# Four transfers for each q, k and v load and two for each quarter of the expert weights, in a fused attention and mixture-of-experts kernel

## The chip, the cores and the metric

The kernel runs on one core of a Trainium2 chip. The metric is the device time of one execution in microseconds (us). Each time stands with the number of executions behind it, and each execution has a state: slow when its time is over 1.5% above the fastest of the same kernel, else fast. Slow runs stay in the medians and ranges quoted, and it is said where there is one. Every time *inside* an execution comes from the one execution of that kernel that was profiled, whose time is some 1.5 to 1.8 us longer than the span that its profile shows; every profiled execution here was a fast one.

The engines are called as in the profile: PE (TensorE, matmul), PEld (its weight loads), DVE (VectorE), ACT (ScalarE), POOL (GpSimd), SP (SyncE, which here only issues transfers). The kernel gives each engine its own list of instructions.

## The reference, cut to what matters

```python
# attention: batch 8, heads 8, seq 576, head_dim 64, 32 landmarks
q_lm = q.reshape(B, H, m, S // m, D).mean(axis=3)      # means over 18 rows each
k_lm = k.reshape(B, H, m, S // m, D).mean(axis=3)
A  = softmax(scale * q @ k_lm.T);  Bm = softmax(scale * q_lm @ k_lm.T);  C = softmax(scale * q_lm @ k.T)
Z  = six Newton steps towards the inverse of Bm
x  = A @ Z @ C @ v                                      # then laid out as (4608, 512)
# mixture of experts: 8 experts, w1 (512 x 1024), w2 (1024 x 512)
e_idx = argmax(x @ w_gate);  gate_w = softmax(x @ w_gate)[e_idx];  eom = sigmoid(x @ w_output_gate)
for e in range(8):
    h = relu(x[mask] @ w1[e]);  out[mask] = gate_w * eom * (h @ w2[e])
```

q, k and v are 32-bit floats, 28 MB in all, and everything else waits for them. The experts' weights are 16-bit in the kernel's memory and 32-bit outside.

## The kernel before

The kernel computes one batch of attention after another, and for each batch it finds the expert that its rows chose, fetches this expert's weights and runs it. When the second of two batches in one weight buffer has chosen the expert that is there already, the fetch is issued under a condition and skipped; on these inputs five experts are fetched and three fetches are skipped. "Expert 0" below is the expert of the first batch, and so on.

A small list scheduler written in the kernel (`Plan`) fixes the order of instructions of every engine when the kernel is built. The change alters none of its inputs, so the order stays.

The loads are issued by SP, one transfer a tensor and batch (two for q and k of the first):

```python
        cuts = ((0, 2), (2, 4)) if b == 0 else ((0, 4),)
        for h, (lo, hi) in enumerate(cuts):
            def ldq(lo=lo, hi=hi):
                nc.sync.dma_start(out=qT.ap[:, lo:hi, :].rearrange("p a s -> p (a s)"), in_=qT_d[ORDER[b]][:, S * lo:S * hi])
        # ... k alike; v in one transfer of 128 rows of 9360 bytes
```

The landmark sums of k are made by DVE ("k sum" below), those of q, but for the first batch, as a tree of five additions by GpSimd ("q tree"; there are seven). GpSimd also reads the number of the chosen expert into a register and issues the weight transfers, four a expert:

```python
            def value(b=b, i8=i8):
                regs[b] = nc.gpsimd.value_load(i8.ap.bitcast(I32)[0:1, 0:1], min_val=0, max_val=E - 1)
    ...
    def fetch(w1t, w2t, reg, k, **kw):                       # one quarter of an expert's weights
        dst = w1t[:, k].rearrange("p a x -> p (a x)") if k < 2 else w2t[:, 4 * k - 8:4 * k - 4].rearrange("p a x -> p (a x)")
        src = w_d[bass.ds(reg, 1)][:, :, 2048 * k:2048 * k + 2048].rearrange("e p x -> p (e x)")
        nc.gpsimd.dma_start(out=dst, in_=src, **kw)
```

The weights are cast on the way: the page's account of 62.05 MB read from memory is what q, k and v (28.5 MB) and 32 weight transfers at 8192 bytes a row make up, where a weight packet writes 4096 bytes. (That account counts the skipped fetches too.) No run here gives these transfers to SP.

Last, the gate values. `coef` may be placed on DVE or GpSimd by the scheduler, `tmp` too, `cmain` is DVE's:

```python
        plan.op(f"co{b0}", [("DVE", 0.26, co("vector")), ("POOL", 0.26 + 0.12 * n, co("gpsimd"))], ...)   # coef
        plan.op(f"tm{b0}", [("DVE", 0.26, tm("vector")), ("POOL", 0.26 + 0.12 * n, tm("gpsimd"))], ...)   # tmp <- coef, sels
        plan.op(f"cm{b0}", [("DVE", 0.24, ...)], ...)                                                    # cmain <- tmp
```

The softmax here doesn't subtract the row's maximum and nothing guards it: scores larger than these inputs give would overflow.

## Time and profile before

| | before |
|---|---|
| time, median of 3 | 192.99 us (192.61 to 194.84; in the ratios below the last counts as slow) |
| profiled execution | 192.17 us, span 190.4 us, granted TensorE clock 0.90 |
| busy share of the span | PE 75%, DVE 68%, ACT 52%, POOL 28% |
| transfers | 375 GB/s over the span, reads and writes, by the account that counts skipped fetches |

The busy shares do not say what limits the kernel, because three stretches with three limits follow one another. The page's second part cuts the span into 40 slices, here of 4.76 us; each digit is a busy share of the slice in tenths. Of the kernel before:

```profile
PE   0087779757959697375999799785976999999940
...
POOL 2039910894830048990000001620400010100000
...
DMA  5999999999999999999701405999999666066752
```

Up to about 90 us the DMA engines are full; q, k and all but the last v arrive until about 71 us, and then the last v (until 80 us) and the first two experts' weights. From 90 us on PE is at 9 in most slices. Between these two lies a stretch in which POOL is busy (the two nines in slices 17 and 18, counted from one, 76 to 86 us) and PE is not (3 and 7 there, 5 in the next). The timeline of that stretch, with start and duration in us, engine, line, and in brackets the idle time of the engine before the instruction and what ended it:

```profile
69.66 1.68 POOL L942 DMA_DIRECT2D w<-in_w_dram  x3 [0.28 <-issue]
72.03 2.26 POOL L942 DMA_DIRECT2D w<-in_w_dram  x4 [0.69 <-issue]
74.31 2.40 POOL L545 TENSOR_TENSOR qa<-qT 128x1152 f32<-128x1152 f32 x1
...
80.19 0.26 POOL L917 TENSOR_TENSOR coef<-mk,gt 128x40 f32<-128x40 bf16 x1
80.41 2.42 POOL L545 TENSOR_TENSOR qa<-qT 128x1152 f32<-128x1152 f32 x1
...
80.99 1.86 DVE L922 TENSOR_SCALAR sels<-iota,ef 128x8 f32<-128x8 f32 x1
82.96 1.26 DVE L926 TENSOR_TENSOR tmp<-coef,sels 128x40 f32<-128x40 f32 x1
84.26 0.20 DVE L931 TENSOR_REDUCE cmain<-tmp 128x5 f32<-128x40 f32 x1
84.37 2.54 DVE L534 TENSOR_REDUCE kx<-kx 128x128 f32<-128x2304 f32 x1
...
87.02 0.75 PE L570 MATMUL psum<-kx,ql 64*32 64x304 f32 x16 [2.53 <-POOL ql L550]
```

Read it as one chain. POOL issues eight weight transfers (one at 68.66 us, and the seven shown), without waiting for any of them. Only then comes the sixth q tree (that of batch 6, counted from 0), then `coef`, and only with `coef` can DVE make `tmp` and `cmain`. The k sum stands behind these on DVE, though its data have long landed (the last k by 68.7 us), and the score matmul of PE, which reads it, starts 0.11 us after its end. The bracket names POOL as the releaser, because the matmul waits for several semaphores and POOL's came last by the profile's count; by the times, the last of its inputs is the k sum (84.37 + 2.54 = 86.91 us). So whatever delays POOL before 80 us delays PE.

### The profile page before, as it was taken

What the parts mean: (1) busy time and instruction counts of PE and PEld (TensorE: products, weight loads), DVE (VectorE), ACT (ScalarE), POOL (GpSimd) and SP (SyncE); (2) the same over time, 40 slices, a digit from 0 to 9 for tenths busy, and PEclk for the clock granted to TensorE, in tenths of its full rate; (3) what the DMA queues carried; (4) which work ended last, traced back from release to release, by engine and by line L of the source; (5) the groups of instructions that cost most, each with busy time, mean ns of one, the idle gap of its engine ahead of it and who ended that gap; (6) DMA issues with size and microseconds to landing.
All of it is one profiled execution on the core that took longest, in us unless ns stands there. A gap on an engine that the chain in (4) does not pass through costs nothing.

```text
span 190.4 us, 7174 instructions
## 1 busy us (share of the span) xinstructions
PE 142.5 (75%) x3013; PEld 79.5 (42%) x3014; DVE 129.7 (68%) x312; ACT 98.5 (52%) x213; POOL 53.4 (28%) x92
## 2 busy tenths in 40 slices
PE   0087779757959697375999799785976999999940
PEld 0033334433527464253344464463443555434320
DVE  6845543697317466898779987677586967927960
ACT  2025824423654327024489668865266667686340
POOL 2039910894830048990000001620400010100000
PEclk9999975995796969667599999999999999999996
DMA  5999999999999999999701405999999666066752
GB/s 175 418 399 406 419 425 396 407 413 400 419 416 405 399 304 259 283 216 211 142 3 67 172 20 214 174 222 215 213 215 213 125 237 247 22 234 248 262 203 55
DMA packets 15636, 48.91 MB, mean 257 GB/s; under 512 B 1648, under 2 KB 2672, under 8 KB 13680
## 3 DMA queue, kind: packets, MB, share of 16 engines
q1 hardware_dynamic: 12576, 37.90, 51.2%
q0 software_dynamic: 2880, 10.49, 28.1%
q8 instruction: 24, 0.39, 0.8%
q14 instruction: 12, 0.10, 0.2%
q10 hardware_dynamic: 144, 0.03, 0.1%
HBM read 62.05 MB, written 9.44 MB: 375 GB/s over the span
## 4 chain that ended last, share of the span: by engine, by line
PE 46%; DMA 15%; DVE 13%; POOL 9%; issue 9%; ACT 4%; POOLq 1%; DVEq 0%
PE psum L1003 15%; DMA qT<-in_q_dram 12%; PE psum L772 6%; PE psum L1009 5%; PE psum L570 4%; POOL qa L548 4%; POOL qa L545 4%; PE psum L576 3%; DMA w<-in_w_dram 3%; PE psum L998 3%; PE psum L608 3%; DVE sab L1056 2%; PE psum L860 2%; PE psum L640 2%; DVE ql L534 1%
## 5 line engine op out<-in xcount | busy, mean ns | idle before, releaser
L942 POOL DMA_DIRECT2D w<-in_w_dram x32 | 11.5, 358 | 88.2 <-PE psum L772 31.8
L1003 PE MATMUL psum<-w,X 128*128 128x512 bf16 x128 | 32.1, 393 | 3.3 <-issue 2.0
L570 PE MATMUL psum<-kx,ql 64*32 64x304 f32 x256 | 16.7, 524 | 16.2 <-DVE kx L534 10.2
L1084 ACT ACTIVATE y<-psum,cmain 128x512 f32<-128x512 f32 (+1 forms) x35 | 21.6, 658 | 7.9 <-PE psum L1009 3.8
L545 POOL TENSOR_TENSOR qa<-qT 128x1152 f32<-128x1152 f32 x7 | 16.9, 2414 | 19.3 <-DMA qT<-in_q_dram 19.0
L534 DVE TENSOR_REDUCE kx<-kx 128x128 f32<-128x2304 f32 (+1 forms) x9 | 20.4, 2277 | 2.5 <-DMA kx<-in_k_dram 2.5
L772 PE MATMUL psum<-cur,Q 32*32 32x96 f32 (+1 forms) x768 | 16.2, 266 | 7.0 <-DVE Q L801 2.9
L1003 PEld LDWEIGHTS <-X 128*128 128x128 f16 x128 | 11.8, 101 | 18.2 <-issue 6.5
L1056 DVE TENSOR_REDUCE sab<-psum 128x4 f32<-128x992 f32 x16 | 18.8, 1182 | 0.0
L586 ACT ACTIVATE Cexp<-psum 128x544 f32<-128x544 f32 x8 | 5.0, 625 | 26.4 <-PE psum L570 26.4
L548 POOL TENSOR_TENSOR qa<-qa 128x512 f32<-128x512 f32 (+2 forms) x21 | 17.4, 830 | 1.6
L1009 PE MATMUL psum<-P,A 128*128 128x512 f16 x64 | 16.4, 380 | 0.8 <-DVE P L1070 0.5
L772 PEld LDWEIGHTS psum<-cur,Q 32*32 32x32 f32 x768 | 9.4, 113 | 16.9 <-DVE Q L801 6.0
L783 ACT COPY cur<-psum 128x384 f32<-128x384 f32 (+1 forms) x23 | 9.4, 417 | 13.7 <-DVE Q L801 9.6
L576 PE MATMUL psum<-qT,kx 64*32 64x288 f32 x256 | 16.1, 512 | 0.4 <-ACT Bx L593 0.4
L705 DVE SCALAR_TENSOR_TENSOR A<-A,lift,psum 128x576 f16<-128x576 f16 x16 | 12.7, 807 | 4.5 <-PE psum L700 4.5
L801 DVE TENSOR_TENSOR Q<-twoI,psum 128x128 f32<-128x128 f32 (+1 forms) x25 | 6.4, 259 | 12.9 <-PE psum L772 7.8
L640 PE MATMUL psum<-vn,CT 128*32 128x65 f32 x512 | 11.6, 252 | 4.0 <-DMA vn<-in_v_dram 2.6
L570 PEld LDWEIGHTS psum<-kx,ql 64*32 64x32 f32 x256 | 4.5, 121 | 21.4 <-DVE kx L534 11.0
L598 ACT ACTIVATE A<-psum 128x576 f16<-128x576 f32 x16 | 10.5, 655 | 5.1 <-PE psum L576 5.1
L998 PE MATMUL psum<-MTd,w 128*128 128x64 f16 x256 | 10.9, 198 | 2.7 <-ACT Bx L593 0.9
L998 PEld LDWEIGHTS <-w 128*128 128x128 f16 x256 | 10.0, 101 | 6.0 <-issue 3.2
(137 smaller groups left out, 240.2 us busy)
## 6 DMA issues: line engine op xcount, KB each, us to landing
w<-in_w_dram POOLq DMA_DIRECT2D x32, 512.0 KB
vn<-in_v_dram SPq DMA_DIRECT2D x8, 1170.0 KB, 18.6
out_dram<-y SPq DMA_DIRECT2D x32, 256.0 KB, 2.2
qT<-in_q_dram SPq DMA_DIRECT2D x7, 1152.0 KB, 13.7
kx<-in_k_dram SPq DMA_DIRECT2D x7, 1152.0 KB, 15.9
qT<-in_q_dram SPq DMA_DIRECT2D x2, 576.0 KB, 4.8
kx<-in_k_dram SPq DMA_DIRECT2D x2, 576.0 KB, 6.9
out_dram<-y SPq DMA_DIRECT2D x16, 64.0 KB, 2.0
```

The lines of the kernel that those rows point to most:

```text
L534: plan.op(f"{what}s{b}.{h}", [("DVE", 0.07 + 0.62 * (hi - lo), lambda lo=lo, hi=hi: nc.vector.tensor_reduce(dst()[:, lo:hi], src()[:, lo:h ...
L545: nc.gpsimd.tensor_tensor(a, x[:, :, :, 0:9], x[:, :, :, 9:18], op=ADD)
L548: nc.gpsimd.tensor_tensor(a[:, :, :, 0:n], a[:, :, :, 0:n], a[:, :, :, n:2 * n], op=ADD)
L570: nc.tensor.matmul(psC[hf].ap[quad(p), par, 0:CH], lhsT=ql.ap[half(par), p, :], rhs=kx.ap[half(par), p, CH * hf:CH * hf + CH], start=True, ...
L576: nc.tensor.matmul(psA[hf].ap[quad(p), par, 0:HS], lhsT=kx.ap[half(par), p, 0:m], rhs=qT.ap[half(par), p, HS * hf:HS * hf + HS], start=Tru ...
L640: nc.tensor.matmul(pV.ap[quad(p), par, 0:D + 1], lhsT=CT.ap[:, par, 128 * c + 32 * p:128 * c + 32 * p + 32], rhs=vn.ap[:, 8 * c + 2 * p + ...
L772: nc.tensor.matmul(it.ap[to, par, 96 * i + lo:96 * i + 96], lhsT=s[:, 0:m] if st == 0 else Q.ap[fr, par, i, :], rhs=s[:, lo:], start=True, ...
L998: nc.tensor.matmul(o, lhsT=weights(b)[0][:, u, q, 128 * fc:128 * fc + 128], rhs=MTd[:, b, q, :].rearrange("p (a x) -> p a x", a=2), start= ...
L1003: nc.tensor.matmul(dst, lhsT=Xt[:, fc, 128 * par:128 * par + 128], rhs=w2t[:, fc, :], start=(fc == 0), stop=(fc == FC - 1))
L1009: nc.tensor.matmul(dst, lhsT=A16[b][:, par, 128 * c:128 * c + 128], rhs=Pt[:, par, :], start=(par == 0), stop=(par == 1))
L1056: nc.vector.tensor_reduce(sab[:, b, f4], x, axis=mybir.AxisListType.XY, op=ADD, apply_absolute_value=True)
L1084: nc.scalar.activation(out=o, in_=x, func=COPY, scale=k)
```

## The change

It cuts every load of q, k and v into four transfers of 295 KB (v: 299 KB) and every quarter of an expert into two, each of 128 rows still. What such a cut can hope for is a consumer that starts with the first piece. No consumer here does: sums and trees read all pieces.

```diff
-                nc.sync.dma_start(out=qT.ap[:, lo:hi, :].rearrange("p a s -> p (a s)"), in_=qT_d[ORDER[b]][:, S * lo:S * hi])
+                for p in range(lo, hi):
+                    nc.sync.dma_start(out=qT.ap[:, p, :], in_=qT_d[ORDER[b]][:, S * p:S * p + S])
     # ... k alike ...
-            nc.sync.dma_start(out=vn.ap.rearrange("p a s -> p (a s)"), in_=v_d[ORDER[b]])
+            for c in range(4):
+                nc.sync.dma_start(out=vn.ap[:, 9 * c:9 * c + 9].rearrange("p a s -> p (a s)"), in_=v_d[ORDER[b]][:, 585 * c:585 * c + 585])
     # ... in fetch() ...
-        nc.gpsimd.dma_start(out=dst, in_=src, **kw)
+        for h in range(2):
+            nc.gpsimd.dma_start(out=dst[:, 1024 * h:1024 * h + 1024], in_=src[:, 1024 * h:1024 * h + 1024], **kw)
```

```
L946 DMACopy w_0_95<-in_w_dram 128x1024
L946 DMACopy w_1_94<-in_w_dram 128x1024 [waits DMASW0_49]
L946 DMACopy w_1_94<-in_w_dram 128x1024 [waits DMASW1_49]
...
L946 DMACopy w_1_96<-in_w_dram 128x1024 [waits DMASW7_49]
```

The trace has the same: expert 1's eight issues each carry a wait for one of eight semaphores, in the order of expert 0's, and SP's transfers take eight in turn as well. Before, experts 0 and 1 were just eight transfers, and none of them waited.

More of the change, by code (lines that the diff above doesn't have):

```diff
@@ L523, in ldk @@
             def ldk(lo=lo, hi=hi):
-                nc.sync.dma_start(out=kx.ap[:, lo:hi, m:], in_=kT_d[ORDER[b]].rearrange("p (a s) -> p a s", a=NP)[:, lo:hi])
+                for p in range(lo, hi):
+                    nc.sync.dma_start(out=kx.ap[:, p, m:], in_=kT_d[ORDER[b]][:, S * p:S * p + S])
             dma(f"ldk{b}.{h}", ldk, kb * (hi - lo) / 4, ("L", b, 0.1 + 0.01 * h), w=[("k", b, h)], new=[] if h else [kx], use=[kx] if h else [])
         def ldv():
-            nc.sync.dma_start(out=vn.ap.rearrange("p a s -> p (a s)"), in_=v_d[ORDER[b]])
+            for c in range(4):
+                nc.sync.dma_start(out=vn.ap[:, 9 * c:9 * c + 9].rearrange("p a s -> p (a s)"), in_=v_d[ORDER[b]][:, 585 * c:585 * c + 585])
         dma(f"ldv{b}", ldv, 128 * 36 * 65 * 4 / 1e3, ("V", b, 0), w=[("v", b)], new=[vn])
```

## The prediction

> **What bounds the kernel now.** From 2 to 71 us the DMA is full (slice row: 9 in every slice, about 400 GB/s): q, k and v stream in order, and the chain of waits holds 17.9 us of "DMA qT" (15.7 to 33.7 us). From about 88 us on PE, fed by in-order DVE and ACT, is the limit (PE 9 in most slices), with 6 us of weight landing at 118. Between them lies the stretch that matters. GpSimd (POOL) issues the weights of experts 0 and 1 (timeline: 8 transfers, 68.7 to 74.3 us, about 0.56 us each), then makes the two last q trees (74.3 to 80.1, 80.4 to 86.2 us), with coef at 80.2 between them. DVE needs that coef for tmp (83.0), then makes the k sum (84.4 to 86.9), and PE's score matmul follows at 87.0 us.

> **Removed:** nothing. No consumer starts earlier: sums and trees read all pieces, and the instruction order of PE, DVE and ACT is unchanged in the build.

> **Added.** (1) Packets. In the packet records 9216 B take 351 ns, 2304 B 95 ns; so q costs 4x95-351 = 29 ns more per row, v about 26. Over 16 engines, with 9 ns per extra completion packet, that is 1.4 us by the fourth q (33.1 us), 2.5 to 3 us by the last k. [...] (2) GpSimd issue: each half still has 128 rows, so I estimate 0.56 us each, double per expert.
> (3) Semaphore slots, the main cost. The build gives each DMA path eight completion semaphores in rotation; a ninth transfer waits until the first has landed. SP stays safe: eight pieces of 0.295 MB are about 5.8 us of queue, above the 1.0 us from issue to first packet. GpSimd does not: before, two experts are exactly eight transfers and it waits for none. After, they are sixteen: expert 1's eighth half waits for expert 0's eighth.

> **On the critical path.** The four quarters of expert 0 landed at 74.2, 79.8, 82.6 and 85.1 us in the completion packets, sharing the engines with the last v. [...] the eighth half lands near 87.5. So GpSimd is free at about 88 instead of 74.3 us; coef comes at 94, the k sum ends at about 99, the score matmul runs near 99 instead of 87.0: +12 us, and everything in order behind it moves along. The same recurs for experts 2 and 3: coef and tmp of their group stand behind six halves of expert 3, each waiting for a half of expert 2; cmain on DVE slips from 124.7 by about 5 us relative, of which 1.3 us is idle now: +4 us. Expert 4 finds slack.

> **Predicted: 208 us**, 8 in 10 between 200 and 215. Faster 0.01, within 2% 0.03, slower 0.96.

> **What would show it.** Timeline of GpSimd: second expert's halves spaced by 1.2 to 2 us, each "<-DMA w", and the sixth q tree starting near 88 us. DVE idle before tmp for some 10 us, released by GpSimd. Packets of 2304 and 2340 B at 95 to 98 ns. DMA still full to about 73 us; if it has holes there, SP's eight slots starve it and my step is wrong. cmain of group (2,3) about 5 us later relative to the load of expert 2.

> **What would make it wrong.** GpSimd's issue being much cheaper or dearer for half rows; the first halves landing sooner because v, now in small packets, takes a smaller share of the engines; slack in DVE or PE after the stall that absorbs part; PE's granted clock rising after a longer idle (now 0.90).

## The result, and the profile after

The changed kernel took 216.69 us (median of 4, 216.12 to 218.16); the kernel before, in the same rounds, 192.8 us (median of 4, one of them slow, 191.32 to 194.84). Ratios here are the mean time of one kernel's fast runs over that of the other's fast runs of the same rounds, so they are not quite the ratio of the medians: it is 1.128, 95% interval 1.1185 to 1.1374. The direction of the prediction held, and so did the mechanism of its largest term; the size did not. 216.7 us lies above the range of 200 to 215 us. All outputs are right.

The slices of the changed kernel are of 5.4 us:

```profile
PE   0094899479878954001899898753959899999900
...
POOL 2049602984503422598000003543150011100000
...
DMA  5999999999999999991000415999999256167560
```

PE now has a hole in slices 17 to 19 (87 to 103 us), a dip in slices 26 to 28 (135 to 152 us), and no work in the last two. DMA is full up to 97 us and has no holes, so SP's own eight semaphores do no harm. The timeline of the hole; these are the instructions shown of before, at line numbers three or four higher:

```profile
68.49 4.61 POOL L946 DMA_DIRECT2D w<-in_w_dram  x8 [10.81 <-DVE e L908]
76.13 0.53 POOL L946 DMA_DIRECT2D w<-in_w_dram  x1 [3.03 <-DMA w<-in_w_dram]
78.15 0.53 POOL L946 DMA_DIRECT2D w<-in_w_dram  x1 [1.49 <-DMA w<-in_w_dram]
...
90.08 0.53 POOL L946 DMA_DIRECT2D w<-in_w_dram  x1 [1.08 <-DMA w<-in_w_dram]
90.63 2.38 POOL L548 TENSOR_TENSOR qa<-qT 128x1152 f32<-128x1152 f32 x1
...
96.30 0.26 POOL L920 TENSOR_TENSOR coef<-mk,gt 128x40 f32<-128x40 bf16 x1
...
96.59 2.34 DVE L929 TENSOR_TENSOR tmp<-coef,sels 128x40 f32<-128x40 f32 x1 [16.07 <-POOL coef L920]
98.96 0.20 DVE L934 TENSOR_REDUCE cmain<-tmp 128x5 f32<-128x40 f32 x1
99.14 2.55 DVE L537 TENSOR_REDUCE kx<-kx 128x128 f32<-128x2304 f32 x1
...
101.79 1.27 PE L573 MATMUL psum<-kx,ql 64*32 64x304 f32 x16 [18.16 <-POOL qa L551]
```

Expert 0's eight halves are issued in 4.61 us, 0.58 us each. Each of expert 1's halves then waits for the landing of one of them ("<-DMA w"; by the trace's semaphore records each starts 0.28 or 0.29 us after the sixteenth count of the semaphore that it waits for), and POOL stands still in between, with a tree and a `coef` to make whose inputs are all there. The tree begins at 90.63 us instead of 74.31, DVE idles 16.07 us, PE 18.16 us. That is the price, in this trace, of eight semaphores and an issuer that works in order: PE had idled 2.53 us there before.

To see where the rest comes from, I matched the 312 instructions of DVE of the two traces one by one (their order is the same) and took how much later each one starts. The shift changes in only a few places:

| place, before | shift of DVE | what DVE or PE waited for there |
|---|---|---|
| k sum, 84.4 us | +14.8 | POOL `coef`, above |
| 105.0 to 118.0 us | +15.2 | nothing more: clock |
| CT copy, 127.6 us | +21.1 | POOL `tmp` behind the halves of experts 2 and 3 |
| 136.4 us | +20.6 | (half a us made up) |
| 146.3 us | +22.4 | the skipped fetch of expert 5 behind expert 4's halves |
| last y, 184.5 us | +23.0 | |
| end of the span, 190.4 us | +26.1 | POOL's end of program |

The second stall has the form of the first, with `coef` and `tmp` of the third group on POOL behind all halves of expert 2 and six of expert 3. First the kernel before, then the changed one:

```profile
117.95 0.59 POOL L942 DMA_DIRECT2D w<-in_w_dram  x1 [31.78 <-PE psum L772]
...
123.80 0.35 POOL L917 TENSOR_TENSOR coef<-mk,gt 128x80 f32<-128x80 bf16 x1
124.23 0.36 POOL L926 TENSOR_TENSOR tmp<-coef,sels 128x80 f32<-128x80 f32 x1
124.66 0.20 DVE L931 TENSOR_REDUCE cmain<-tmp 128x10 f32<-128x80 f32 x1
128.88 0.31 PE L679 MATMUL psum<-A,sel 128*32 128x144 f16 x8 [0.35 <-DVE CT L623]
...
138.95 0.05 POOL L942 DMA_DIRECT2D w<-in_w_dram  x1 [0.83 <-DMA w<-in_w_dram]
```

```profile
133.15 0.59 POOL L946 DMA_DIRECT2D w<-in_w_dram  x1 [30.93 <-PE psum L775]
133.95 0.53 POOL L946 DMA_DIRECT2D w<-in_w_dram  x1 [0.21 <-issue]
...
145.78 0.53 POOL L946 DMA_DIRECT2D w<-in_w_dram  x1 [0.71 <-DMA w<-in_w_dram]
146.33 0.35 POOL L920 TENSOR_TENSOR coef<-mk,gt 128x80 f32<-128x80 bf16 x1
147.14 0.24 DVE L934 TENSOR_REDUCE cmain<-tmp 128x10 f32<-128x80 f32 x1 [7.34 <-POOL tmp L929]
149.95 0.43 PE L682 MATMUL psum<-A,sel 128*32 128x144 f16 x8 [6.44 <-DVE CT L626]
...
161.10 0.53 POOL L946 DMA_DIRECT2D w<-in_w_dram  x1 [0.25 <-issue]
162.15 0.05 POOL L946 DMA_DIRECT2D w<-in_w_dram  x1 [0.52 <-DMA w<-in_w_dram]
162.21 0.23 PE L1002 MATMUL psum<-MTd,w 128*128 128x64 f16 x2 [1.82 <-DMA w<-in_w_dram]
```

`cmain` comes 22.5 us later than before (147.14 against 124.66), and PE's matmul behind it 21.1 us later. Here most of the delay is not waiting for landings. From the first transfer of expert 2 to `coef` POOL takes 5.85 us before, with seven transfers ahead of `coef`, and 13.18 us after, with fourteen (133.15 to 146.33). These fetches carry a condition, and where nothing holds them they start 0.78 us apart, before and after alike; seven more are 5.5 of the 7.3 us. Only the last four of the six halves wait for a landing (each is issued 0.6 us after it), which adds 1.5 us to the gaps between issues.

The last three lines are the third wait. The instruction of 0.05 us is a skipped fetch: it moves nothing, but it stands in POOL's order behind expert 4's eight halves, and PE waits for it as for a weight. It is 23.2 us later than before (162.15 against 138.95), so a little more than everything around it. No landing holds the eight halves here: they start 0.78 us apart, each 3.1 us or more after the half that it would have to wait for has landed, so what the skipped fetch stands behind is their issuing.

The end of the program has no compute instructions and so is not in the timeline; these are the records of the trace there, in us:

| | before | after |
|---|---|---|
| last y on DVE starts | 184.45 | 207.41 |
| POOL's semaphore increment for its transfers | 185.98, lasts 0.59 | 211.38, lasts 0.99 |
| POOL's drain | 186.59 to 188.30 | 212.40 to 215.74 |
| SP ready for the last barrier | 189.64 | 213.14 |
| POOL answers the barrier | 189.67 | 215.78 |
| end of span | 190.4 | 216.6 |

Before, POOL is done 1.3 us ahead of SP, which waits for output transfers. After, SP is ready first and waits for POOL. From the last y to the end it takes 6.0 us before and 9.2 us after.

### The profile page after: what moved, and what is told of

Same layout as the page of the kernel before. It is cut to its first block, busy times and chain, and to the rows that moved or that the text cites. A ratio compares the mean times of both kernels' runs of the same rounds, so it can differ in the third digit from the quotient of the medians.

```text
span 216.6 us, 7433 instructions
## 1 busy us (share of the span) xinstructions
PE 145.9 (67%) x3013; PEld 80.0 (37%) x3014; DVE 130.4 (60%) x312; ACT 98.6 (46%) x213; POOL 64.3 (30%) x124
## 5 line engine op out<-in xcount | busy, mean ns | idle before, releaser
L946 POOL DMA_DIRECT2D w<-in_w_dram x64 | 22.5, 353 | 97.0 <-DMA w<-in_w_dram 39.7
L573 PE MATMUL psum<-kx,ql 64*32 64x304 f32 x256 | 17.3, 551 | 34.5 <-POOL qa L551 18.2
L1007 PE MATMUL psum<-w,X 128*128 128x512 bf16 x128 | 33.7, 409 | 1.4 <-DVE sab L1060 1.3
L775 PE MATMUL psum<-cur,Q 32*32 32x96 f32 (+1 forms) x768 | 15.5, 262 | 6.0 <-DVE Q L804 3.3
L1051 ACT ACTIVATE X<-psum,mr 128x256 f16<-128x256 f32 x28 | 11.0, 479 | 9.9 <-DVE sab L1060 7.8
L643 PE MATMUL psum<-vn,CT 128*32 128x65 f32 x512 | 13.3, 259 | 2.9 <-DMA vn<-in_v_dram 1.4
L804 DVE TENSOR_TENSOR Q<-twoI,psum 128x128 f32<-128x128 f32 (+1 forms) x25 | 6.4, 258 | 11.1 <-PE psum L775 5.6
```

What stands on the lines that cost most here:

```text
L573: nc.tensor.matmul(psC[hf].ap[quad(p), par, 0:CH], lhsT=ql.ap[half(par), p, :], rhs=kx.ap[half(par), p, CH * hf:CH * hf + CH], start=True, ...
L643: nc.tensor.matmul(pV.ap[quad(p), par, 0:D + 1], lhsT=CT.ap[:, par, 128 * c + 32 * p:128 * c + 32 * p + 32], rhs=vn.ap[:, 8 * c + 2 * p + ...
L775: nc.tensor.matmul(it.ap[to, par, 96 * i + lo:96 * i + 96], lhsT=s[:, 0:m] if st == 0 else Q.ap[fr, par, i, :], rhs=s[:, lo:], start=True, ...
L946: nc.gpsimd.dma_start(out=dst[:, 1024 * h:1024 * h + 1024], in_=src[:, 1024 * h:1024 * h + 1024], **kw)
L1007: nc.tensor.matmul(dst, lhsT=Xt[:, fc, 128 * par:128 * par + 128], rhs=w2t[:, fc, :], start=(fc == 0), stop=(fc == FC - 1))
```

## The experiments

Theory S (slots): the loss comes from the number of transfers on GpSimd's path; with more than eight in flight, GpSimd waits for landings, and what stands behind it in GpSimd's order waits too. Rivals: P (packets): half-size packets and more of them slow the transfers themselves, weights or q, k and v. I (issue): GpSimd's 0.56 us a transfer is simply spent twice as often.

### Each half of the change alone

`e1_w_halves_only` keeps q, k and v whole and has the change in `fetch` only; `e2_qkv_only` has the other half only. Their diffs are the parts of the diff above.

> Weights in halves, q, k and v as before. Slots theory (sixteen halves wait for eight completion slots, and GpSimd, which issues them in order, stands still): nearly the whole loss, 212 to 215 us, GpSimd's q tree of batch 6 starting near 88 us, DVE idle about 14 us before tmp. Load theory (the loss comes from q, k and v cut small, or from SP waiting for its slots): 194 to 200 us. Packet theory (smaller packets and twice the issue work): about half the loss, 203 to 207.

> q, k and v in four transfers each, weights as before. Slots theory: 193 to 196 us, the last k landing about 3 us later but GpSimd's second expert still issued without a wait near 74 us. Load theory: 210 or more. Packet theory: about half the loss, 203 to 207.

With the weight halves alone 214.0 us (median of 4, 213.31 to 214.84; ratio 1.1106, interval 1.1015 to 1.1196). With q, k and v alone 192.95 us (median of 4, 192.23 to 193.71; ratio 0.9988, interval 0.9912 to 1.0064), in rounds where the kernel before had 192.75 us (median of 7, one of them slow). The cut of q, k and v, alone, costs nothing that these runs can show, though its last k lands 3.1 us later (71.8 against 68.7 us, by the sixteenth count of its semaphore). POOL in `e2_qkv_only` issues expert 1 without a wait, as before:

```profile
71.80 2.26 POOL L945 DMA_DIRECT2D w<-in_w_dram  x4 [0.72 <-DVE ef L903]
74.07 2.42 POOL L548 TENSOR_TENSOR qa<-qT 128x1152 f32<-128x1152 f32 x1
```

So rival P falls for q, k and v. The whole change loses 23.9 us in medians and the weights alone 21.3, which leaves 2.6 us for the two together: with q, k and v in pieces the last v's share the engines longer with expert 0's weights (their pieces land up to 89.2 us), and POOL's eight waits end at 90.1 us instead of 87.3.

### Small weight packets without more transfers

`e3_two_packets_a_row` keeps q, k and v whole and four transfers an expert, but pads each weight tile in the middle of its row, so that every row of a transfer becomes two packets of 2048 bytes, as in the changed kernel.

```diff
-    w1 = [keep.tile([128, 2, NP, F // 2], F16, name=f"w1_{s}") for s in range(2)]
-    w2 = [keep.tile([128, FC, HD], BF16, name=f"w2_{s}") for s in range(2)]
+    w1 = [keep.tile([128, 2, 2, F + 8], F16, name=f"w1_{s}") for s in range(2)]
+    w2 = [keep.tile([128, FC // 2, 2 * HD + 8], BF16, name=f"w2_{s}") for s in range(2)]
     # fetch: dst and src as [128, 2, 1024]; the matmuls index the padded tiles; no more transfers
```

> q, k, v as before; four weight transfers per expert as before, but the tile has a gap in each row, so each transfer has two packets of 2048 B (written) per row, as the halves have: 256 rows per issue, the small packets, but still eight transfers for two experts and no slot wait. Slots theory: 193 to 197 us (the issue of 256 rows may cost more than 0.56 us). Packet theory: as e1_w_halves_only, over 205.

193.21 us (median of 4, 192.49 to 194.59; ratio 1.0001, interval 0.9926 to 1.0077). The packet records show 5120 weight packets of 2048 bytes with a median of 173 ns, which is what the changed kernel has, and the time is that of before.

```profile
70.68 3.15 POOL L942 DMA_DIRECT2D w<-in_w_dram  x4 [16.06 <-DVE e L905]
74.06 2.87 POOL L942 DMA_DIRECT2D w<-in_w_dram  x4 [0.23 <-issue]
76.92 2.43 POOL L545 TENSOR_TENSOR qa<-qT 128x1152 f32<-128x1152 f32 x1
```

Rival P falls for the weights as well. The rows are dearer to issue (0.72 to 0.79 us a transfer, against 0.56), and the tree is 2.6 us later, of which nothing is seen in the median; the profiled execution was itself the slowest of the four.

### How many transfers wait, and at which expert

In these three, `fetch` learns for which expert it works:

```diff
-    def fetch(w1t, w2t, reg, k, **kw):
+    def fetch(w1t, w2t, reg, k, b=None, **kw):
-        nc.gpsimd.dma_start(out=dst, in_=src, **kw)
+        n = 2 if b == 0 else 1                    # e8: expert 0 alone in halves
+        # e4: n = 2 if b in (0, 1) else 1         # experts 0 and 1
+        # e5: n = 2 if b is not None and b > 1 else 1   # all but these
+        for h in range(n):
+            o = 2048 // n
+            nc.gpsimd.dma_start(out=dst[:, o * h:o * h + o], in_=src[:, o * h:o * h + o], **kw)
```

> Dose: expert 0 in halves, all others in quarters, so twelve transfers for the first two experts and the last waits for the fourth half, not the eighth. Slots theory: in e1_w_halves_only the fourth half let GpSimd go on about 5 us before the eighth, so GpSimd is free near 82.8 us and the loss is 12.4 less 5, 7 to 8 us: 199 to 202 us. Packet theory: 8 of 64 halves, 195.

> Only the weights of the first two experts in halves, everything else as before. Slots theory: the first stall alone, plus 12 to 13 us (in e1_w_halves_only PE's shift after it was 12.4 us), 204 to 207 us. If every half costs alike (packet theory), 16 of the 64 halves would give a quarter of the 21 us, 198.

> Only the weights of the third and later experts in halves. Slots theory: the stall of cmain of batches 2 and 3 (6 us in PE's shift of e1_w_halves_only), about 1 us behind expert 4, and the longer tail after the last store: 199 to 203 us. If every half costs alike: three quarters of the 21 us, 208.

The kernel before had 193.2 us in these rounds (median of 7). `e8_expert0_only`: 201.15 us (median of 4, 200.03 to 201.63; ratio 1.0386, interval 1.0323 to 1.045). `e4_first_pair`: 205.94 us (204.33 to 206.87; 1.0629, 1.0546 to 1.0711). `e5_later`: 202.6 us (202.05 to 203.55; 1.0497, 1.0434 to 1.056).

With the runs above, these put zero, four or eight waiting transfers ahead of the sixth q tree. Times in us, from the traces:

| run | transfers of experts 0 and 1 | of which wait | q tree starts | score matmul starts | difference |
|---|---|---|---|---|---|
| before | 8 | 0 | 74.31 | 87.02 | 12.7 |
| e2_qkv_only | 8 | 0 | 74.07 | 87.91 | 13.8 |
| e3_two_packets_a_row | 8, of 256 rows | 0 | 76.92 | 89.66 | 12.7 |
| e8_expert0_only | 12 | 4 | 82.89 | 93.98 | 11.1 |
| e1_w_halves_only | 16 | 8 | 87.79 | 98.86 | 11.1 |
| e4_first_pair | 16 | 8 | 88.10 | 99.18 | 11.1 |
| after | 16 | 8 | 90.63 | 101.79 | 11.2 |

PE follows POOL's tree at a distance that varies little (in `e2_qkv_only` `coef` itself waits another 1.19 us for DVE), and the tree follows the number of waits. For this first stall rival I falls by size: twelve transfers are four more than before, 2.2 us at 0.56 us each, but the tree is 8.6 us later in `e8_expert0_only`. For the second and third place it does not fall: there the issuing, at 0.78 us a transfer, is the larger part, as the times above show. No run separates issuing from waiting there. PE is 1.6 us nearer to the tree in the four with waits, because DVE finished `sels` during the wait in 0.23 us; before, `sels` took 1.86 us beside a running tree (more of this below).

The two parts add up to within a microsecond: `e4_first_pair` costs 12.7 us and `e5_later` 9.4 us in medians, 22.1 together, against 21.3 for `e1_w_halves_only`. In `e5_later` the first stretch is as before (shift +0.6 us), the second place costs +6.0 us (0.6 to 6.6) and the third +1.8 (6.2 to 8.0).

### The same transfers, placed elsewhere

If POOL's order is the cause, the sixteen transfers should be harmless behind the work that others wait for. A helper run after the scheduler moves them in the order; it asserts that each operation still stands behind what it depends on, so no wait was removed by hand.

```diff
+    def later(names, mark):                       # takes these operations out and puts them behind mark
+        ...
+    later(["er1"] + [f"ldw1.{k}" for k in range(4)], "co0")      # move 1: expert 1 behind the first coef
+    later(["er3"] + [f"ldw3.{k}" for k in range(3)], "tm2")      # move 2, in e7: expert 3's first three quarters behind tmp
```

`e6_after_move1` is the changed kernel with move 1, `e7_after_move12` with both.

> The changed kernel, but GpSimd issues expert 1's weights after the q tree of batch 6 and coef, not before; all other engines in the same order. Slots and in-order theory: the first stall goes, coef near 80 us, score matmul of batch 6 near 84 to 88 us, time 216.7 less 14 to 16, so 200 to 203 us; the later stall (cmain of batches 2 and 3, about 7 us) stays. Packet and load theories: 214 to 218, nothing changes, since the same bytes and packets move.

> The changed kernel with two moves on GpSimd: expert 1's weights behind the q tree of batch 6 and coef, and expert 3's behind coef and tmp of batches 2 and 3. Same bytes, packets and slots, only what stands behind the waiting halves changes. Slots and in-order theory: both stalls go, 193 to 197 us. Packet and load theories: no better than e6_after_move1, 200 or more.

`e6_after_move1`: 200.64 us (median of 4, 199.46 to 202.49, one of them slow; ratio 1.0383, interval 1.0267 to 1.0498), 16 us under the changed kernel with the very same transfers and packets (the same move takes nearly 3 us off the kernel before as well, `f1_before_move1` below). The timeline of it shows the tree and `coef` ahead, and the waits behind:

```profile
69.28 4.61 POOL L946 DMA_DIRECT2D w<-in_w_dram  x8 [12.65 <-DVE e L908]
73.91 2.43 POOL L548 TENSOR_TENSOR qa<-qT 128x1152 f32<-128x1152 f32 x1
...
82.23 0.26 POOL L920 TENSOR_TENSOR coef<-mk,gt 128x40 f32<-128x40 bf16 x1 [2.55 <-DVE gt L917]
83.41 2.83 POOL L946 DMA_DIRECT2D w<-in_w_dram  x5 [0.93 <-issue]
86.89 0.53 POOL L946 DMA_DIRECT2D w<-in_w_dram  x1 [0.64 <-DMA w<-in_w_dram]
```

The score matmul starts at 86.44 us, 0.6 us *before* that of the kernel before, and DVE is 2.6 us ahead at 118 us. The first stall is gone, and the second is untouched (shift −2.6 to +3.4 us).

`e7_after_move12`: 198.28 us (median of 4, 197.9 to 199.79; ratio 1.027, interval 1.0195 to 1.0345, so whether it is slower by 2% is unclear). I had expected 193 to 197 us, and it missed. The second stall is indeed gone, DVE is 4.7 us ahead at 136 us, but then PE stops for the third wait, which was 1.8 us in the changed kernel and is now long:

```profile
142.02 0.05 POOL L946 DMA_DIRECT2D w<-in_w_dram  x1 [0.52 <-DMA w<-in_w_dram]
142.07 0.29 PE L1002 MATMUL psum<-MTd,w 128*128 128x64 f16 x2 [6.38 <-DMA w<-in_w_dram]
```

The skipped fetch of expert 5 stands behind expert 4's halves, and these now wait, one by one, for expert 3's halves, which move 2 had put just ahead of them: each is issued 0.6 or 0.7 us after one of those has landed. DVE's shift goes from −4.7 to +2.5 us. The wait that was taken out of one place in the rotation of eight came back at the next eight transfers. The other part of the miss is the end of the program, which takes 10.1 us from the last y on instead of 6.0 in the kernel before.

`e9_move12_expert4_whole` tests this reading: it is `e7_after_move12` with expert 4's quarters whole again.

```diff
+        n = 1 if b == 4 else 2
```

> The changed kernel with both moves, and expert 4's quarters whole (experts 0 to 3 still in halves, q, k and v in pieces). Theory (after the two moves, what is left of the loss is expert 4's eight halves, each waiting for a half of expert 3, with expert 5's skipped fetch behind them, plus the longer end of GpSimd): no wait of 6 us for weights on PE near 138 us, PE 2 to 4 us ahead of the kernel before up to the end, the final drain about 3.0 us, in all 190 to 193 us against 198.3 with the halves. Rival (the third wait is the landing of expert 3's and 4's data itself, whatever the number of transfers): 196 to 199 us, the wait on PE still there.

192.42 us (median of 4, 191.08 to 193.89; ratio 0.9993, interval 0.9921 to 1.0064; the kernel before had 193.84 us in these rounds, median of 11, one of them slow). Four transfers fewer save 5.9 us of the median. The skipped fetch now comes six us earlier than in `e7_after_move12`, in the timeline:

```profile
135.96 0.05 POOL L948 DMA_DIRECT2D w<-in_w_dram  x1 [0.52 <-DMA w<-in_w_dram]
```

Of the waits of PE and PEld for weights, that of 6.38 us is gone, and the list of waits (total us, times, longest us) has one of about 1 us left on each:

```profile
PEld L1004 <- DMA w<-in_w_dram: 1.0, 1, 1.0
PE psum L1004 <- DMA w<-in_w_dram: 0.9, 1, 0.9
```

DVE keeps its lead of 3.6 us to the last y, the end of the program then takes 8.7 us instead of 6.0, and 190.4 − 3.6 + 2.7 = 189.5 us is the span that the profile shows. The loss of the change is thus accounted for: three places where work stood behind transfers on GpSimd (behind their waiting at the first, mostly behind their issuing at the other two), and the end. That this run is level with the kernel before is a sum of two things: the moves gain there too (`f3_before_move12` below, 1.3%), and the longer end costs as much.

### The end of the program

The drain (POOL's long DRAIN record near the end of the trace, 1.71 us before and 3.34 us after) was not the subject of a run of its own, but the twelve runs vary what it seems to depend on. From the trace records, by the number of transfers that GpSimd really made:

| transfers | runs | increment, us | drain, us | last y to end, us |
|---|---|---|---|---|
| 20 | before, e2, e3, f1, f2, f3 | 0.59 | 1.71 | 5.8 to 6.5 |
| 24 | e8 | 0.67 | 2.18 | 7.6 |
| 28 | e4 | 0.75 | 2.36 | 7.9 |
| 32 | e5 | 0.83 | 2.69 | 8.1 |
| 36 | e9 | 0.92 | 3.01 | 8.7 |
| 40 | after, e1, e6, e7 | 0.99 | 3.34 | 9.1 to 10.1 |

About 0.08 us of drain and 0.02 of increment a transfer. Rows or packets do not count: `e3_two_packets_a_row` has as many weight packets as the changed kernel and drains in 1.71 us. Part of the longer end stays open: with 28 transfers and more, POOL also needs 3.2 to 4.4 us, instead of 1.0, from its last register load to the increment, and no run separates why.

### Does the finding help the kernel before?

Four issues of 0.56 us stand ahead of the tree in the kernel before too. `f1_before_move1` is the kernel before with move 1, `f2_qkv_move1` has q, k and v in pieces as well, `f3_before_move12` is the kernel before with both moves. The edits are the lines shown above.

> The kernel before with whole quarters; only expert 1's four transfers stand later on GpSimd, behind the sixth q tree and coef. Theory (GpSimd's order is what the first stretch waits for, even in the kernel before, where four issues of about 0.56 us stand ahead of the tree): coef near 77.5 us, the score matmul 1 to 3 us before 87.0, PE some 2 to 4 us ahead until the second group; if that lead survives to the end, 189 to 191 us (ratio 0.98 to 0.99). Rival (GpSimd is not what holds the end of the kernel before: expert 1's weights land later, or the later groups wait for their own weights): 192 to 194 us with the lead lost at a DMA wait.

> q, k and v in four transfers each, whole weight quarters, and expert 1's four transfers behind coef. Theory (the q, k and v cut is free when nothing on GpSimd waits): same as the run with the move alone, within 0.5 us. Rival (the cut costs some 2 us of transfer that the wait for coef hid): 1 to 2.5 us more than the move alone.

> The kernel before with both moves (expert 1's transfers behind the first coef, expert 3's behind the second tmp), whole quarters. Theory: in the kernel before expert 3's three first quarters are issued without a full round of waits, so the second move gains at most 1 us over the first move alone: 188.5 to 190.5 us. Rival (expert 3's weights then come too late and PE waits for them): 191 to 194 us.

`f1_before_move1`: 189.77 us (median of 6, 188.87 to 192.42, one of them slow; ratio 0.9871, interval 0.9815 to 0.9927), with the kernel before at 192.5 us (median of 11, two of them slow). `f2_qkv_move1`: 190.3 us (median of 6, 188.47 to 191.03; 0.9896, 0.9837 to 0.9956). `f3_before_move12`: 190.48 us (median of 6, 189.02 to 191.0; 0.987, 0.9821 to 0.9919), with the kernel before at 193.84 us.

All three beat the kernel before by 1.0 to 1.3%, with an interval that excludes no gain. The second move adds nothing that these runs can show. Between `f2_qkv_move1` and `f1_before_move1` lies 0.5 us, less than the two intervals (about 1.1 us each) can resolve: a cost of 2.5 us of the q, k and v cut is excluded, one of 1 us is not.

The gain of move 1 did not come the way I had expected. `coef` is not at 77.5 us but later than before, since its own input comes late from DVE; what is gained is gained on DVE:

```profile
81.78 0.26 POOL L917 TENSOR_TENSOR coef<-mk,gt 128x40 f32<-128x40 bf16 x1 [4.75 <-DVE gt L914]
...
82.59 0.23 DVE L922 TENSOR_SCALAR sels<-iota,ef 128x8 f32<-128x8 f32 x1
82.92 0.20 DVE L926 TENSOR_TENSOR tmp<-coef,sels 128x40 f32<-128x40 f32 x1
```

`sels` takes 0.23 us instead of 1.86 and `tmp` 0.20 instead of 1.26, 2.7 us less for the same work, and no tree runs on POOL beside them. In the changed kernel `tmp` runs beside the seventh tree and takes 2.34 us. It is not a slowdown in proportion: in all 18 cases in the traces where `sels` or `tmp` took more than 0.4 us, it ended 0.02 to 0.07 us after the end of the addition on POOL that ran beside it (before: `sels` at 82.86 and the addition at 82.83 us, `tmp` at 84.23 and 84.17). So in these traces how long it takes depends on how much of that addition is still to come; why, no run shows.

## Why the prediction was right or wrong

**Right: the sign, and the mechanism of the first stall.** Expert 1's halves wait for expert 0's, each "<-DMA w", 1.6 to 2.7 us apart (predicted 1.2 to 2); `coef` stands behind them; DVE idles before `tmp` (16.07 us, predicted some 10); DMA has no holes; SP's eight semaphores do no harm; a half of experts 0 and 1 costs POOL 0.53 to 0.58 us (predicted 0.56). The moves show that this order is the cause: the same transfers behind `coef` take 16 us off.

**Near in size, and off the critical path: packets.** Packets of 2304 and 2340 bytes have means of 98.8 and 100.6 ns, medians of 93 and 95 (predicted 95 to 98, from medians before), and the last k lands 4.0 us later in the changed kernel, at 72.7 us, and 3.1 us later in `e2_qkv_only` (predicted 2.5 to 3). This delay did not reach PE, which was 0.6 us early at 83.8 us, and q, k and v in pieces cost nothing in the run that had them alone. The smaller pieces do show in the bandwidth: from 10 to 60 us the changed kernel moves 387 GB/s against 408. It was the wrong place to look for time here.

**Wrong: the landing of the eighth half, the cost of the later halves, and one term that was missing.** The prediction's terms add to 16 us over 192.99 us, and I wrote 208. The medians differ by 23.9 us. Between the two profiled spans it is 26.1 us, because the changed kernel's profiled execution was the slowest of its four; the steps below add to that:

| step, as the prediction put it | predicted | measured | why |
|---|---|---|---|
| "the score matmul runs near 99 instead of 87.0: +12" | +12 | +14.8, then +15.2 | "the eighth half lands near 87.5", POOL free at 88; it landed at 89.8 and POOL was free at 90.6 |
| experts 2 and 3: "cmain ... slips ... by about 5 us relative ... +4 us" | +4 | +5.9 | DVE waited 7.3 us, not 5; "each waiting" was wrong: issuing seven more transfers at 0.78 us made up 5.5 of it, waiting less than 2 |
| "Expert 4 finds slack" | 0 | +1.8 | expert 5's skipped fetch stands behind the issuing of its halves |
| the rest of the way to the last y | 0 | 0.0 | half a us made up, half a us lost |
| end of the program | not considered | +3.2 | drain and increment grow with the number of transfers |

The first term was mis-sized in the landing. The sixteenth count of the semaphore of expert 0's eighth half came at 89.80 us, 2.3 us after the 87.5 that I had estimated, and POOL went on 0.28 us later. The sixteen counts of that half are spread over 2.9 us, from 86.91 us on. My estimate rested on sorting the completion packets of all engines sixteen to a transfer, and this hides the spread: that way the eighth landing would be at 88.1 us. What POOL went on after, in all eight waits, was the slowest of the sixteen counts. I had also let one v overlap expert 0's weights, where in small pieces both of the last two did (their pieces land between 74.8 and 89.2 us): with q, k and v whole (`e1_w_halves_only`) the eighth half lands at 86.97 us and POOL is free at 87.8 us, just where I had it. `tmp` beside a tree (2.34 us) costs the first term 1.1 us more than before, which the earlier end of `sels` more than gives back.

"Expert 4 finds slack" failed because I looked at when its data are needed, and not at what stands behind it in POOL's order. The same place costs 0.3 us in `e1_w_halves_only`, where the halves again start 0.78 us apart, and 7.2 us in `e7_after_move12`, where each waits for a landing; with expert 4 whole it costs nothing.

**The clock.** I had put a rising clock after a longer idle among what could make me wrong. It fell, from 0.90 to 0.84. The profile's windows of clock 0.5 from 74 us to the last y are 78.9 to 82.3, 85.7 to 109.6, 147.2 to 154.0 and 164.2 to 167.6 us after the change, and 77.4 to 84.3 and 87.7 to 94.5 us before. The shortest of them last 3.4 us. Ahead of the one from 147.2 us PE had been idle since 143.5 us. The others begin otherwise: by the modelled matmul times PE was busy for 39% of the 3.4 us ahead of 85.7 us and for 65% of those ahead of 77.4 us. What sets this clock these runs do not show. The clock added little: the score matmul took 1.27 us in such a window against 0.75 at full clock before, but at the first stall the shift grows by 0.4 us (14.8 to 15.2), since the kernel before ran that same stretch at half clock too.

## What to carry to other kernels

Before cutting a transfer into pieces, count the transfers that are in flight at once on one issuing path against the number of its completion semaphores (eight here), and ask what stands behind the issuer in its order: the packets cost nothing that the runs could show here (ratios 0.9988 and 1.0001), and a full rotation cost 15 us in one place. Count the issuing itself too: at the second place seven more transfers at 0.78 us were most of the 5.9 us lost. When the issuer is an engine that computes, place transfers behind the work that others wait for, and follow the rotation to its next round, since a wait removed in one place can come back eight transfers on, as it did in `e7_after_move12`. Conditional fetches that move nothing wait in the same line and are waited for like real ones: PE waited 1.82 us for one whose issue takes 0.05 us, and 6.38 us in `e7_after_move12`.
